# Weight transfers on SyncE's queue, and two streams of preparation for the second MLP

## The chip, the cores and the metric

One core of a Trainium2 chip runs the kernel. The metric is device time in microseconds (us), the median of several executions. The engines: TensorE (PE in the profile; PEld is its weight load), VectorE (DVE), ScalarE (ACT), GpSimd (POOL) and SyncE (SP), which only issues transfers. A small q behind an engine's name (ACTq, SPq) marks its sequencer, which issues DMAs and waits.

## The reference

```python
p_packed = sm_attn(p, k, v)            # 8 batches, 8 heads, 32 packed rows over 576 keys, d = 64
out = sm_attn(q, p_packed, p_packed)   # 576 queries over the 32 packed rows
x = out.transpose(0, 2, 1, 3).reshape(4608, 512)
h = x @ w_in;  g = h * sigmoid(h);            x = g @ w_out        # first MLP, 512 -> 2048 -> 512
h = x @ w_in2; g = h * clip(h + 3, 0, 6) / 6; return g @ w_out2    # second MLP, same sizes
```

All of it is float32. The kernel gets float32 accuracy out of faster matmuls: it splits each operand into a high and a low float32r part and adds three products.

## The kernel before

**Blocks.** The 4608 tokens are nine blocks (j = 0 to 8) of 512. For blocks 1 to 7 the hidden layer of the first MLP is computed from the attention weights and from "fused" weights (packed values times w_in, `fuse_steps`, L607), whose products run beside the blocks before: each step takes one product out of a PSUM bank (L616 to L618), and ScalarE (L622) and VectorE (L623) split it. In each block (`block`, L854) a loop over the 16 columns f of the hidden layer does twelve or six matmuls (L827 to L829), the Silu gate on ScalarE (L835), a split of it by ScalarE (gh, L842) and VectorE (gl, L843), and the projection of the column two before (L850 to L852). Attention steps for later blocks are placed among these by a planner (`Plan`), by costs and due times. A block ends with its sums being copied out of PSUM and stored (x1d, L896).

**Weights.** Block 0 converts the first MLP's weights from raw words (`Feed`: L173, L174 on ScalarE, L179, L180 on VectorE, L185 and a split on GpSimd) and keeps them in DRAM as w1i and w1o. Later blocks load them: wi tiles (`next_in`, L215) with five buffers, wo tiles (`next_out`, L228) with three. ScalarE issues both. The attention's loads (nat, tails of q, k and v, p), x1d and xtd are issued by SyncE.

**Preparation.** `Prep` (L243) makes the second MLP's weights in Strassen-like form: 32 units, each with two loads of raw words (L263), two conversions (L173, L174), bit work on VectorE (L179, L180), an addition on GpSimd (L292), four VectorE sums (L295 to L298), two rounding copies on ScalarE (L300, L301), two subtractions on GpSimd (L303, L304), and three stores to w2 (L308 to L310). ScalarE issues loads and stores. It is a generator: `prep.step()` does the work up to the next `yield`. A unit has nine of them, some with nothing between. `nxt` calls it from block 1 on: twice per column in blocks 1 to 6 (32 steps a block), 46 times in block 7 and 62 times in block 8.

**The second MLP** (`Second`, L918) follows block 8. Its weight loads (ws) and its first x loads (xr) are issued by SyncE; the first of them in block 8.

Every engine works through its own list of instructions in the order of the program, and waits where an operand or a buffer isn't ready. All DMAs take eight landing counters in turn, whichever queue issues them: a DMA waits on its issuing engine until the one eight before it has landed.

Of the kernel before, what the change touches and what calls it, by code (L numbers as in the profile page):

```python
# [1 line left out]

# [6 lines left out]
F32 = mybir.dt.float32  # L9
I32 = mybir.dt.int32  # L10
U32 = mybir.dt.uint32
F32R = mybir.dt.float32r
# [6 lines left out]
def tile_pack_attention_two_mlps(ctx: ExitStack, tc, q, k, v, p, w_in1, w_out1, w_in2, w_out2, out):  # L19
# [8 lines left out]
    nc = tc.nc  # L28
# [141 lines left out]
    def conv_begin(key, room=ring):  # L170
        raw = raws.pop(key).rearrange("p (f t) -> p f t", t=2)
        r, t = room(), room().bitcast(I32)
        nc.scalar.mul(out=r, in_=f32(raw[:, :, 1]), mul=2.0 ** -112)  # L173
        nc.scalar.mul(out=t, in_=raw[:, :, 0].bitcast(U32), mul=2.0 ** -29)  # L174
        raws[key] = raw[:, :, 1], r.bitcast(I32), t
# [32 lines left out]
    def piece_in(f):  # L208
        return w1i[f // GF][:, :, :, f % GF, :].rearrange("c p n f -> p n c f")
# [5 lines left out]
    def next_in():  # L215
        if want_in:
            key = want_in.pop(0)
            t = wts.tile([P, 2, DM], F32R, tag="wi", name="wi", bufs=5)
            if len(key) == 3:
                j, g, c = key  # L220
                nc.scalar.dma_start(out=f32(t).rearrange("p n (i f) -> p n i f", i=GF), in_=w1i[g][c])
            else:
                nc.scalar.dma_start(out=f32(t).rearrange("p n (c f) -> p n c f", c=KC), in_=piece_in(key[1]))
            have_in[key] = t

    projected = [-1, -1]
# [1 line left out]
    def next_out():  # L228

        now, projected[1] = projected[1], -1 if kept else projected[0]  # L230
        while want_out and now >= NF - 2 and (want_out[0][0] * NF + want_out[0][1]) // 2 <= (now + 1) // 2 - 1 + WO:
            j, f = want_out.pop(0)
            t = half_w("out", f)
            nc.scalar.dma_start(out=f32(t), in_=w1o[f].rearrange("n p f -> p n f"))
            have_out[j, f] = t


# [5 lines left out]
    class Prep:  # L243


        def __init__(self, pool, w_in, w_out_):
            self.pool = pool
            self.src = {"in": lambda f: win_src(w_in, f), "out": lambda f: wout_src(w_out_, f)}
            self.units = [(kind, f, h) for kind in ("in", "out") for f in range(HF) for h in range(2)]
            self.steps = self.all()  # L250

        def room(self):
            return self.pool.tile([P, T], F32, tag="pring", name="pr", bufs=4)

        def load(self, u):

            kind, f, h = self.units[u]
            raw = self.pool.tile([P, 2 * T], I32, tag="praw", name="praw", bufs=2)
            for n, to in enumerate(raw.rearrange("p (n r) -> n p r", n=2)):
                src = self.src[kind](f + n * HF)  # L260
                if kind == "out":
                    src = src.rearrange("p a (r f) -> p (a r) f", r=4)
                nc.scalar.dma_start(out=to.rearrange("p (r f) -> p r f", r=2), in_=src[:, h:4:2])  # L263
            raws["p", u] = raw

        def step(self):
            next(self.steps, None)

        def end(self):
            for _ in self.steps:  # L270
                pass

        def all(self):
            self.load(0)
            for _ in range(6):
                yield
            for u, (kind, f, h) in enumerate(self.units):
                key = "p", u
                c = self.pool.tile([P, 8, P], F32, tag="c8", name="c8")
                hi = self.pool.tile([P, S7, P], F32, tag="hi7", name="hi7", bufs=2)  # L280
                conv_begin(key, self.room)
                yield
                yield
                conv_bits(key)
                yield
                if u + 1 < len(self.units):
                    self.load(u + 1)
                yield
                x, r = (t.rearrange("p (n r f) -> p n r f", n=2, r=2) for t in raws.pop(key))
                a = c[:, 0:4].bitcast(I32)  # L290
                a = a.rearrange("p (n r) f -> p n r f", n=2) if kind == "in" else a.rearrange("p (r n) f -> p n r f", n=2)
                nc.gpsimd.tensor_add(out=a, in0=x, in1=r)  # L292
                yield

                nc.vector.tensor_add(out=c[:, 4], in0=c[:, 2], in1=c[:, 3])  # L295
                nc.vector.tensor_sub(out=c[:, 6], in0=c[:, 0], in1=c[:, 2])
                nc.vector.tensor_sub(out=c[:, 5], in0=c[:, 4], in1=c[:, 0])
                nc.vector.tensor_sub(out=c[:, 7], in0=c[:, 1], in1=c[:, 5])  # L298
                yield
                nc.scalar.copy(out=hi[:, 0:2].bitcast(F32R), in_=c[:, 0:2])  # L300
                nc.scalar.copy(out=hi[:, 2:7].bitcast(F32R), in_=c[:, 3:8])  # L301
                yield
                nc.gpsimd.tensor_sub(out=c[:, 0:2].bitcast(F32R), in0=c[:, 0:2], in1=hi[:, 0:2])  # L303
                nc.gpsimd.tensor_sub(out=c[:, 3:8].bitcast(F32R), in0=c[:, 3:8], in1=hi[:, 2:7])  # L304
                yield
                yield
                to = w2[kind][f].rearrange("s p f -> p s f")
                nc.scalar.dma_start(out=to[:, :, h * P:(h + 1) * P], in_=hi)  # L308
                nc.scalar.dma_start(out=to[:, 0:2, (2 + h) * P:(3 + h) * P], in_=c[:, 0:2])
                nc.scalar.dma_start(out=to[:, 2:7, (2 + h) * P:(3 + h) * P], in_=c[:, 3:8])  # L310


    AHEAD = 3
# [3 lines left out]
    def load_tail(n, what):  # L317
        src = {"k": k, "q": q, "v": v}[what]
        b, h0 = n // QPB, (n % QPB) * HQ
        if n == 1 and what != "v":  # L320
            t = half_kb(n, f"{what}t")[0:TAIL, 0:HQ * D].rearrange("p (h d) -> p h d", h=HQ)
        else:
            t = at.tile([TAIL, HQ, D], F32, tag=f"{what}t", name=f"{what}t")
        nc.sync.dma_start(out=t, in_=src[b, h0:h0 + HQ, T:S, :].rearrange("h s d -> s h d"))
        nat[what, n] = t

    def load_nat(n, what, j):
        src = {"k": k, "q": q, "v": v}[what]
        b, h0 = n // QPB, (n % QPB) * HQ + 2 * j
        m = half_kb(n, "nat", 2 * AHEAD, what)  # L330
        rows = src[b, h0:h0 + 2, 0:T, :]
        if what == "v":
            m = m.rearrange("p (h i d) -> p h i d", h=2, i=NI)
            nc.sync.dma_start(out=m.rearrange("p h i d -> p h (i d)"), in_=rows.rearrange("h (p i) d -> p h (i d)", i=NI))
        elif n >= 4:

            g = m.rearrange("p (i b d) -> p i b d", i=NI, b=NI)
            for h in range(2):
                for e in range(2):
                    o = (2 * h + e) * NP  # L340
                    nc.sync.dma_start(out=g[o:o + NP], in_=rows[h].rearrange("(b r i) d -> r i b d", b=NI, i=NI)[:, :, :, e * NP:(e + 1) * NP])
        else:
            m = m.rearrange("p (i h d) -> p i h d", h=2, i=NI)
            for h in range(2):
                nc.sync.dma_start(out=m[:, :, h, :], in_=rows[h].rearrange("(p i) d -> p i d", i=NI))
            m = m.rearrange("p i h d -> p i (h d)")
        nat[what, n, j] = m
# [10 lines left out]
    def spread_p(n):  # L358
        if ("pbd", n) in st:
            return  # L360
        pn = nat.pop(("p", n))
        pbd = at.tile([P, HQ, D], F32, tag="pbd", name="pbd")
        nc.gpsimd.tensor_tensor(out=pbd, in0=pn.to_broadcast([P, HQ, D]), in1=mask.to_broadcast([P, HQ, D]), op=ALU.mult)
        st["pbd", n] = pbd
# [904 lines left out]
    d2s[1] = spare_raw()[:, 0:S]  # L1269
    feed.ahead = RAW - 2  # L1270

    load_nat(0, "k", 0)
    load_tail(0, "q")
    feed.load()
    load_p(0)
    load_tail(0, "k")
    spread_p(0)
    load_nat(0, "k", 1)
    load_tail(1, "q")
    load_tail(1, "k")  # L1280
# [73 lines left out]
    for j in range(NBLK):  # L1354
# [34 lines left out]

        if j == 1:  # L1390
            first_block.close()
            prep = Prep(opened(first_left, "prep"), w_in2, w_out2)
        if j == NBLK - 1:
            first_right.close()
# [4 lines left out]
        def nxt(f, full, j=j):  # L1399
            if j == 0:  # L1400
                if full:
                    feed.advance()
                    calls[0] += 1
                    if 20 <= calls[0] < 25:
                        next_in()
                else:
                    feed.begin()
            else:
                if j >= B - 1 or full:
                    prep.step()  # L1410
                if full and j == B:
                    mlp2.begin_step()
# [52 lines left out]
```

## Time and profile before

| | |
|---|---|
| median of 3 runs | 1669.15 us (1660.82 to 1673.3) |
| profiled execution | 1664.09 us, span 1662.3 us, mean granted clock 0.982 |
| TensorE, VectorE, ScalarE, GpSimd busy | 1559.9, 1047.3, 806.2, 215.1 us |
| transfers by queue | q1 250.68 MB (50.6% of the DMA engines' time), q10 135.81 MB (25.9%) |
| start; block 0 | 0 to 46; to 176.5 us |
| blocks 1 to 8 | to 298, 400.5, 486.5, 589, 695.5, 763.5, 830.5, 924.5 us |
| second MLP | 924.5 to 1662.3 us |

Busy time of an engine is the time in which an instruction of it runs; issuing and waiting don't count. The granted clock is the share of 2.4 GHz that TensorE got. The bounds of the blocks are the ends of the copies of their sums.

### The profile page before, as it was taken

Reading aid. Unit: us, or ns where it says so; the run is one execution under the profiler, and the core shown is the slowest. Engines: PE = TensorE matmul, PEld = TensorE weight load, DVE = VectorE, ACT = ScalarE, POOL = GpSimd, SP = SyncE. Lnnn points to the kernel's source line nnn. Section 1 sums busy time; section 2 is a strip of 40 time slices with the busy share of each in tenths; the row PEclk is TensorE's granted clock in tenths of the full one; section 3 lists DMA queues with packets and bytes.
Section 4 is the critical chain, followed back from the end, with each engine's and each line's share of the span. In section 5 each row is a group of like instructions: output and inputs, shape, how many; then the busy total and the mean of one; then the engine's idle time right before and its main releaser. Section 6 shows DMA issues by size and latency. Waiting matters only on the chain.

```text
span 1662.3 us, 23562 instructions
## 1 busy us (share of the span) xinstructions
PE 1559.9 (94%) x8396; PEld 1339.8 (81%) x8396; DVE 1047.3 (63%) x1750; ACT 806.2 (48%) x1356; POOL 215.1 (13%) x188
## 2 busy tenths in 40 slices
PE   5888899889998999999999999999999999999997
PEld 3566666567676777668878999999999999999997
DVE  5678454655556545664443579579578678687675
ACT  4776444545455444555434345345344444453443
POOL 2455011101111112112223000000000000000000
PEclk9999999999998999999999999999999999999999
DMA  7888695867676764856598687888887888888885
GB/s 195 265 258 276 196 233 151 250 192 212 158 217 188 205 188 116 270 174 210 179 307 264 210 267 252 253 299 253 262 290 252 270 285 253 278 272 253 262 255 166
DMA packets 409750, 388.01 MB, mean 233 GB/s; under 512 B 156193, under 2 KB 282145, under 8 KB 409633
## 3 DMA queue, kind: packets, MB, share of 16 engines
q1 hardware_dynamic: 281200, 250.68, 50.6%
q10 hardware_dynamic: 128432, 135.81, 25.9%
q8 instruction: 68, 1.11, 0.3%
q14 instruction: 50, 0.40, 0.1%
HBM read 324.53 MB, written 61.87 MB: 232 GB/s over the span
## 4 chain that ended last, share of the span: by engine, by line
PE 57%; DVE 17%; ACT 14%; DMA 6%; issue 3%; ACTq 2%; POOL 1%; SPq 0%; DVEq 0%; POOLq 0%
PE b L1169 6%; PE b L1170 6%; PE b L1168 6%; PE acc L850 6%; PE acc L851 5%; PE acc L852 5%; ACT hr L1029 4%; DVE g L1032 4%; PE hps L827 3%; PE hps L829 3%; PE hps L828 3%; PE b L1086 2%; PE b L1084 2%; PE b L1085 2%; DVE fused L623 1%
## 5 line engine op out<-in xcount | busy, mean ns | idle before, releaser
L1169 PE MATMUL b<-ro,ws 128*128 128x384 f32 x672 | 226.5, 337 | 6.2 <-DVE ro L1128 6.2
L1084 PE MATMUL b<-xc,ws 128*128 128x384 f32 x672 | 228.9, 341 | 3.0 <-DVE hv L1048 2.1
L1170 PE MATMUL b<-ro,ws 128*128 128x384 f32 x672 | 225.9, 336 | 0.0
L1168 PE MATMUL b<-ro,ws 128*128 128x384 f32 x672 | 225.8, 336 | 0.0
L1086 PE MATMUL b<-xc,ws 128*128 128x384 f32 x672 | 225.0, 335 | 0.0
L1085 PE MATMUL b<-xc,ws 128*128 128x384 f32 x672 | 224.7, 334 | 0.0
L843 DVE TENSOR_TENSOR gl<-hps,gh 128x512 fp32r<-128x512 f32 x144 | 99.0, 687 | 188.6 <-ACT gh L842 185.5
L1123 ACT CAST ro<-g 128x768 fp32r<-128x768 f32 x168 | 138.3, 835 | 101.9 <-DVE g L1117 36.6
L1128 DVE TENSOR_TENSOR ro<-g,ro 128x768 fp32r<-128x768 f32 x168 | 158.5, 951 | 8.9 <-ACT ro L1123 7.5
L1169 PEld LDWEIGHTS b<-ro,ws 128*128 128x128 f32 x672 | 126.3, 188 | 8.1 <-DVE ro L1128 8.1
L1084 PEld LDWEIGHTS b<-xc,ws 128*128 128x128 f32 x672 | 126.2, 188 | 7.3 <-DVE hv L1048 4.4
L835 ACT ACTIVATE hps<-hps 128x512 f32<-128x512 f32 x144 | 84.0, 583 | 92.6 <-PE hps L829 74.8
L1085 PEld LDWEIGHTS b<-xc,ws 128*128 128x128 f32 x672 | 126.3, 188 | 0.0
L1170 PEld LDWEIGHTS b<-ro,ws 128*128 128x128 f32 x672 | 126.3, 188 | 0.0
L1168 PEld LDWEIGHTS b<-ro,ws 128*128 128x128 f32 x672 | 126.3, 188 | 0.0
L1086 PEld LDWEIGHTS b<-xc,ws 128*128 128x128 f32 x672 | 126.1, 188 | 0.0
L850 PE MATMUL acc<-gh,wr 128*128 128x512 f32 x288 | 119.4, 414 | 1.3 <-ACT gh L842 1.3
L850 PE MATMUL acc<-gh,wo 128*128 128x512 f32 x288 | 117.0, 406 | 2.3 <-ACT gh L842 2.3
L851 PE MATMUL acc<-gl,wr 128*128 128x512 f32 x288 | 114.7, 398 | 0.2 <-DVE gl L843 0.2
L852 PE MATMUL acc<-gh,wr 128*128 128x512 f32 x288 | 114.2, 397 | 0.0
L851 PE MATMUL acc<-gl,wo 128*128 128x512 f32 x288 | 113.4, 394 | 0.2 <-DVE gl L843 0.2
L852 PE MATMUL acc<-gh,wo 128*128 128x512 f32 x288 | 113.3, 393 | 0.0
(262 smaller groups left out, 3048.1 us busy)
## 6 DMA issues: line engine op xcount, KB each, us to landing
ws<-w2in SPq DMA_DIRECT2D x336, 256.0 KB, 4.1
ws<-w2out SPq DMA_DIRECT2D x336, 256.0 KB, 3.4
wi<-w1i ACTq DMA_DIRECT2D x80, 512.0 KB, 4.8
wo<-w1o ACTq DMA_DIRECT2D x64, 512.0 KB, 5.2
x1d<-x SPq DMA_DIRECT2D x18, 512.0 KB, 2.9
w1i<-win SPq DMA_DIRECT2D x16, 512.0 KB, 6.0
praw<-in_moe_w_in_dram ACTq DMA_DIRECT2D x32, 256.0 KB, 5.5
praw<-in_moe_w_out_dram ACTq DMA_DIRECT2D x32, 256.0 KB, 4.8
```

The costliest lines, as they stand in the source:

```text
L843: nc.vector.tensor_sub(out=gl, in0=g, in1=f32(gh))
L850: mm(acc[e], lhsT=w[:, 0, s], rhs=gh, start=first, stop=False)
L851: mm(acc[e], lhsT=w[:, 0, s], rhs=gl, start=False, stop=False)
L852: mm(acc[e], lhsT=w[:, 1, s], rhs=gh, start=False, stop=last)
L1084: mm(ps, lhsT=wh, rhs=xs[k][:, 0, c], start=first, stop=False, skip_group_check=True)
L1085: mm(ps, lhsT=wh, rhs=xs[k][:, 1, c], start=False, stop=False, skip_group_check=True)
L1086: mm(ps, lhsT=wl, rhs=xs[k][:, 0, c], start=False, stop=last, skip_group_check=True)
L1123: nc.scalar.copy(out=t[:, 0], in_=self.operand(s))
L1128: nc.vector.tensor_sub(out=t[:, 1], in0=self.operand(s), in1=f32(t[:, 0]))
L1168: mm(acc[i], lhsT=wh, rhs=ro[:, 0, f], start=first, stop=False, skip_group_check=True)
L1169: mm(acc[i], lhsT=wh, rhs=ro[:, 1, f], start=False, stop=False, skip_group_check=True)
L1170: mm(acc[i], lhsT=wl, rhs=ro[:, 0, f], start=False, stop=last, skip_group_check=True)
```

## The change

All transfers of weights that ScalarE issued after block 0's raw loads (wi, wo, the raw words and the stores of the preparation) are issued by SyncE. wi has four buffers instead of five, and block 0 asks for four tiles early instead of five. The preparation is two generators, one for the even and one for the odd units, with buffers of their own; `step` advances them in turn. A unit still has nine `yield`s, now each with something between them. The preparation begins with block 2 and takes two more steps per column in block 7 (78 in all). The first loads at the start have another order, p first, and the tail of q gets a second buffer.

```diff
 def next_in():
-            t = wts.tile([P, 2, DM], F32R, tag="wi", name="wi", bufs=5)
+            t = wts.tile([P, 2, DM], F32R, tag="wi", name="wi", bufs=4)
-                nc.scalar.dma_start(out=f32(t).rearrange("p n (i f) -> p n i f", i=GF), in_=w1i[g][c])
+                nc.sync.dma_start(out=f32(t).rearrange("p n (i f) -> p n i f", i=GF), in_=w1i[g][c])
...
 def next_out():
-            nc.scalar.dma_start(out=f32(t), in_=w1o[f].rearrange("n p f -> p n f"))
+            nc.sync.dma_start(out=f32(t), in_=w1o[f].rearrange("n p f -> p n f"))
...
 class Prep:
-            self.steps = self.all()
-
-        def room(self):
-            return self.pool.tile([P, T], F32, tag="pring", name="pr", bufs=4)
+            self.steps = [self.all(first) for first in range(2)]
+            self.turn = 1
...
-            raw = self.pool.tile([P, 2 * T], I32, tag="praw", name="praw", bufs=2)
+            raw = self.pool.tile([P, 2 * T], I32, tag=f"praw{u % 2}", name="praw")
...
-                nc.scalar.dma_start(out=to.rearrange("p (r f) -> p r f", r=2), in_=src[:, h:4:2])
+                nc.sync.dma_start(out=to.rearrange("p (r f) -> p r f", r=2), in_=src[:, h:4:2])
...
         def step(self):
-            next(self.steps, None)
+
+            self.turn = 1 - self.turn
+            next(self.steps[self.turn], None)
...
-        def all(self):
-            self.load(0)
-            for _ in range(6):
+        def all(self, first):
+            room = lambda: self.pool.tile([P, T], F32, tag=f"pring{first}", name="pr", bufs=2)
+            mine = range(first, len(self.units), 2)
+            self.load(first)
+            for _ in range(4):
                 yield
...
-                conv_begin(key, self.room)
-                yield
+                conv_begin(key, room)
                 yield
                 conv_bits(key)
                 yield
-                if u + 1 < len(self.units):
-                    self.load(u + 1)
-                yield
+                if u + 2 < len(self.units):
+                    self.load(u + 2)
...
                 nc.vector.tensor_sub(out=c[:, 6], in0=c[:, 0], in1=c[:, 2])
+                yield
                 nc.vector.tensor_sub(out=c[:, 5], in0=c[:, 4], in1=c[:, 0])
...
                 nc.gpsimd.tensor_sub(out=c[:, 0:2].bitcast(F32R), in0=c[:, 0:2], in1=hi[:, 0:2])
+                yield
                 nc.gpsimd.tensor_sub(out=c[:, 3:8].bitcast(F32R), in0=c[:, 3:8], in1=hi[:, 2:7])
                 yield
+                to = w2[kind][f].rearrange("s p f -> p s f")
+                nc.sync.dma_start(out=to[:, :, h * P:(h + 1) * P], in_=hi)
+                nc.sync.dma_start(out=to[:, 0:2, (2 + h) * P:(3 + h) * P], in_=c[:, 0:2])
+                nc.sync.dma_start(out=to[:, 2:7, (2 + h) * P:(3 + h) * P], in_=c[:, 3:8])
                 yield
-                yield
-                to = w2[kind][f].rearrange("s p f -> p s f")
-                nc.scalar.dma_start(out=to[:, :, h * P:(h + 1) * P], in_=hi)
-                nc.scalar.dma_start(out=to[:, 0:2, (2 + h) * P:(3 + h) * P], in_=c[:, 0:2])
-                nc.scalar.dma_start(out=to[:, 2:7, (2 + h) * P:(3 + h) * P], in_=c[:, 3:8])
...
-    load_nat(0, "k", 0)
-    load_tail(0, "q")
-    feed.load()
     load_p(0)
     load_tail(0, "k")
+    load_tail(0, "q")
+    load_nat(0, "k", 0)
     spread_p(0)
+    feed.load()
...
         if j == 1:
             first_block.close()
+        if j == 2:
             prep = Prep(opened(first_left, "prep"), w_in2, w_out2)
...
-                    if 20 <= calls[0] < 25:
+                    if 20 <= calls[0] < 24:
                         next_in()
...
-                if j >= B - 1 or full:
+                if j > 1 and (j >= B - 1 or full):
+                    prep.step()
+                if j == B - 1 and full:
                     prep.step()
```

## Rows read from the trace of the kernel before

**Rows 1.** Busy time by stretch: bounds, length, engines (instructions), clock, DMA share, GB/s.
```profile
176.50:298.00 121.50, 107.94 (x609) 74.91 (x608) 58.92 (x124) 57.24 (x98) 14.90 (x17) 0.97 0.77 206
298.00:400.50 102.50, 91.04 (x465) 67.18 (x464) 57.69 (x114) 52.85 (x91) 13.60 (x12) 0.95 0.75 211
400.50:486.50 86.00, 84.75 (x461) 63.75 (x460) 47.89 (x101) 44.98 (x79) 16.56 (x17) 1.00 0.66 178
486.50:589.00 102.50, 91.92 (x460) 67.22 (x459) 57.30 (x114) 51.84 (x89) 13.08 (x12) 0.93 0.76 209
...
695.50:763.50 68.00, 65.11 (x278) 49.86 (x278) 40.49 (x74) 36.07 (x58) 8.38 (x7) 0.97 0.63 201
763.50:830.50 67.00, 67.00 (x295) 54.83 (x294) 25.70 (x53) 33.65 (x60) 20.07 (x17) 1.00 0.63 201
830.50:924.50 94.00, 89.91 (x386) 72.81 (x385) 35.76 (x65) 38.48 (x65) 23.05 (x18) 0.98 0.85 261
924.50:1662.30 737.80, 719.92 (x4172) 712.56 (x4170) 539.98 (x799) 324.30 (x515) 14.18 (x6) 1.00 0.81 260
```

**Rows 2.** TensorE's waits, blocks 1 to 8: releaser, us in total, times, longest.
```profile
PE hps L827 <- DVE gl L843: 9.3, 4, 4.6
PE abank L616 <- issue: 9.3, 6, 2.9
PE acc L850 <- ACT gh L842: 3.6, 2, 2.3
PE abank L406 <- ACT gh L842: 3.5, 1, 3.5
...
PE abank L478 <- DVE ppf L465: 2.7, 2, 1.9
PE abank L616 <- DVE gl L843: 2.6, 1, 2.6
...
PE abank L461 <- DVE a1Tt L104: 1.6, 1, 1.6
PE hps L827 <- DVE xh L623: 1.5, 1, 1.5
```

**Rows 3.** ScalarE's timeline early in block 2: start, length, idle time before.
```profile
298.99 0.38 ACTq L308 DMA_DIRECT2D w2in<-hi  x1
299.46 1.36 ACTq L309 DMA_DIRECT2D w2in<-c  x1
300.91 1.24 ACTq L310 DMA_DIRECT2D w2in<-c  x1
302.19 0.66 ACT L173 ACTIVATE pr<-praw 128x512 f32<-128x512 f32 x1 [2.63 <-issue]
...
303.30 0.56 ACT L622 CAST fused<-abank 64x512 fp32r<-64x512 f32 x1
```

**Rows 4.** ScalarE's waits, blocks 1 to 8.
```profile
ACT pr L173 <- issue: 37.3, 17, 4.9
...
ACT hi L301 <- DVE c L298: 20.3, 18, 1.4
...
ACT gh L842 <- DMA w2out<-c: 3.6, 1, 3.6
```

**Rows 5.** GpSimd's instructions of the preparation, by tile: ns shortest/median/longest.
```profile
L292 POOL TENSOR_TENSOR c<-pr x32: 1263/1288/1782, 206.6 to 907.6; 128x512 int32<-128x512 int32 x32
...
L304 POOL TENSOR_TENSOR c<-c,hi x32: 1548/1569/2092, 222.6 to 910.8; 128x640 fp32r<-128x640 f32 x32
```

**Rows 6.** SyncE's own waits, whole span.
```profile
SPq L324 <- PE abank L461: 94.6, 10, 17.8
```

**Rows 7.** DMA issues of the page: count, KB each, median us to landing.
```profile
wi<-w1i ACTq DMA_DIRECT2D x80, 512.0 KB, 4.8
wo<-w1o ACTq DMA_DIRECT2D x64, 512.0 KB, 5.2
```

**Rows 8.** TensorE's waits in the start, 0 to 46 us.
```profile
PE abank L372 <- POOL pbd L363: 9.1, 1, 9.1
```

More of the change, by code (lines that the diff above doesn't have):

```diff
@@ L1 @@
 from contextlib import ExitStack
+from itertools import zip_longest
 import concourse.bass as bass
@@ L217, in next_in @@
             key = want_in.pop(0)
-            t = wts.tile([P, 2, DM], F32R, tag="wi", name="wi", bufs=5)
+            t = wts.tile([P, 2, DM], F32R, tag="wi", name="wi", bufs=4)
             if len(key) == 3:
                 j, g, c = key
-                nc.scalar.dma_start(out=f32(t).rearrange("p n (i f) -> p n i f", i=GF), in_=w1i[g][c])
+                nc.sync.dma_start(out=f32(t).rearrange("p n (i f) -> p n i f", i=GF), in_=w1i[g][c])
             else:
-                nc.scalar.dma_start(out=f32(t).rearrange("p n (c f) -> p n c f", c=KC), in_=piece_in(key[1]))
+                nc.sync.dma_start(out=f32(t).rearrange("p n (c f) -> p n c f", c=KC), in_=piece_in(key[1]))
             have_in[key] = t
@@ L262, in load @@
                     src = src.rearrange("p a (r f) -> p (a r) f", r=4)
-                nc.scalar.dma_start(out=to.rearrange("p (r f) -> p r f", r=2), in_=src[:, h:4:2])
+                nc.sync.dma_start(out=to.rearrange("p (r f) -> p r f", r=2), in_=src[:, h:4:2])
             raws["p", u] = raw
         def step(self):
-            next(self.steps, None)
+            self.turn = 1 - self.turn
+            next(self.steps[self.turn], None)
         def end(self):
-            for _ in self.steps:
+            for both in zip_longest(*self.steps):
                 pass
-        def all(self):
-            self.load(0)
-            for _ in range(6):
+        def all(self, first):
[3 more added lines that the diff above has]
+            for _ in range(4):
                 yield
-            for u, (kind, f, h) in enumerate(self.units):
+            for u in mine:
+                kind, f, h = self.units[u]
                 key = "p", u
-                c = self.pool.tile([P, 8, P], F32, tag="c8", name="c8")
-                hi = self.pool.tile([P, S7, P], F32, tag="hi7", name="hi7", bufs=2)
-                conv_begin(key, self.room)
-                yield
+                c = self.pool.tile([P, 8, P], F32, tag=f"c8{first}", name="c8")
+                hi = self.pool.tile([P, S7, P], F32, tag=f"hi7{first}", name="hi7")
+                conv_begin(key, room)
                 yield
@@ L285, in all @@
                 yield
-                if u + 1 < len(self.units):
-                    self.load(u + 1)
-                yield
-                x, r = (t.rearrange("p (n r f) -> p n r f", n=2, r=2) for t in raws.pop(key))
+                if u + 2 < len(self.units):
+                    self.load(u + 2)
+                r, t = (v.rearrange("p (n r f) -> p n r f", n=2, r=2) for v in raws.pop(key))
                 a = c[:, 0:4].bitcast(I32)
                 a = a.rearrange("p (n r) f -> p n r f", n=2) if kind == "in" else a.rearrange("p (r n) f -> p n r f", n=2)
-                nc.gpsimd.tensor_add(out=a, in0=x, in1=r)
+                nc.gpsimd.tensor_add(out=a, in0=r, in1=t)
                 yield
@@ L322, in load_tail @@
         else:
-            t = at.tile([TAIL, HQ, D], F32, tag=f"{what}t", name=f"{what}t")
+            t = at.tile([TAIL, HQ, D], F32, tag=f"{what}t", name=f"{what}t", bufs=2 if what == "q" else 1)
         nc.sync.dma_start(out=t, in_=src[b, h0:h0 + HQ, T:S, :].rearrange("h s d -> s h d"))
```

## The prediction

> **What bounds the kernel now.** I first read the stretches block by block [rows 1]. The second MLP (924.5 to 1662.3 us) keeps TensorE at full clock and 98% busy, and the change touches nothing that it issues; I leave it at 738 us. Block 0 and the start change in details only. So the question is the 748 us of blocks 1 to 8. There the reader is to see two kinds of blocks. Blocks 3 and 7 are full: 84.75 us busy of 86, 67.00 of 67. Blocks 1, 2, 4, 6 and 8 are not: TensorE is busy 107.94 of 121.5, 91.04 of 102.5, 91.92 of 102.5, 65.11 of 68 and 89.91 of 94, and the granted clock there is 0.97, 0.95, 0.93, 0.97 and 0.98, a mixture of the two levels of 1.2 and 2.4 GHz. Idle time is 13.6 + 11.5 + 10.6 + 2.9 + 4.1 = 42.7 us in these five, and the clock loses (1 - c) times the stretch, 3.6 + 5.1 + 7.2 + 2.0 + 1.9 = 19.8 us. This is the whole pot: some 62 us.
>
> Next the waits of TensorE in these blocks [rows 2]: none is for a transfer. It waits for ScalarE and VectorE: to have a PSUM bank emptied, or an operand split. The group of 9.3 us at L616 with the releaser "issue" names nobody, so I went to the times of its six cases and read ScalarE's timeline before each. The largest one stands for the pattern [rows 3]: from 298.99 ScalarE issues the three stores of a preparation unit, 0.38, 1.36 and 1.24 us, converts the next raw tile, and only then, at 303.30, evicts the bank that the next product of the fused weights needs; TensorE had nothing to do for 2.9 us, the longest case of that group. Then ScalarE's own waits [rows 4]: it stood 37.3 us before L173, the first instruction behind those stores, because of its own issuing, and 20.3 us before L301 for a VectorE instruction that the preparation had issued one step earlier. Both queues share eight landing counters, each of which must be down before it is used again, so ScalarE also stood for transfers of others: 3.6 us before a Silu's split for the landing of a store.
>
> **The change part by part.** (1) *Issuing leaves ScalarE.* In blocks 1 to 8 ScalarE issues wi, wo, the raw tiles and the stores; an issue costs it 0.38 to 1.36 us in [rows 3]. I price it by TensorE's idle time behind it, group by group [rows 2]: L616 behind issuing 9.3; L616 behind gl 2.6 (gl behind a Silu's split that stood for the landing of xtd); L850 behind gh 3.6 (the split that stood for a store, in block 8 [rows 4]); L406 behind gh 3.5 (in block 1, behind three wo issues in a row); L827 behind xh 1.5. Sum 20.5 us. Of the 9.3 us at L827 behind gl, the two long cases, up to 4.6, come out of a VectorE chain that starts behind such a ScalarE stall; I take a third, 3 us.
>
> (2) *Preparation leaves block 1.* A unit took nine steps, now it takes nine of its stream's, and the streams alternate; block 1 had 32 steps, so some 3.5 units of 32 go elsewhere. Their conversions stood directly ahead of L461 behind a1Tt (1.6) and of the 1.9 of the 2.7 us behind ppf [rows 2]: 3.5 us, nothing takes their place.
>
> (3) *The clock.* The low stretches in blocks 1, 2, 4, 6 and 8 follow idle times of 2.3 to 4.6 us. I take half of the 19.8 us, 9.9, since about half of the long idle times are among those of (1).
>
> (4) *What is late next.* With ScalarE on time, the bank still waits for VectorE's half of the split, and VectorE is already second in the list of waits. In the pattern of [rows 3] the eviction could have begun 2.5 us sooner and the gap was 2.93, so a sixth remains there; where chains are longer more does. I give back a third of (1) and (3), (20.5 + 3 + 9.9) / 3 = 11.1 us.
>
> (5) *Denser preparation in block 7.* Steps there go from 46 to 78: about 3.6 units more. A unit's two long GpSimd instructions take 1.29 and 1.57 us [rows 5], with the short one some 3.6 in all; ScalarE spends on a unit four conversions like the 0.66 us of L173 [rows 3], some 2.5, and VectorE about as much. Block 7 has 20.07 us of GpSimd, 33.65 of ScalarE and 25.70 of VectorE in 67 [rows 1], so 13, 9 and 9 us more fit beside TensorE. A step now comes every 67 / 78 = 0.86 us and one of the same stream every 1.7 us, about as long as the longest GpSimd instruction, so an in-order VectorE may stand for it; Silu's split runs two columns of work ahead and covers that. Bounds: 0, and 13 us if TensorE paid for all of GpSimd; I take 1. Counted out, the two streams need 2 x (4 + 16 x 9) = 296 steps and there are 5 x 32 + 78 + 62 = 300, so nothing is left over at the end of block 8.
>
> (6) *SyncE takes the transfers.* It must keep its order, and it does stand still, up to 17.8 us for one load of a tail [rows 6]. What counts is whether it comes to a weight transfer later than ScalarE did. The eight landing counters are taken in turn in program order, which gives the order of both queues' transfers; laid out so, SyncE had passed the transfer ahead of a wi load too late in 7 of 80 cases [rows 7], by at most an estimated 2.1 us. These waits are for things at the same place of the program, and ScalarE comes there last. The second buffer for q's tail removes one more such wait. Cost 0. (7) *wi with four buffers instead of five, four early loads instead of five:* a load lands in 4.8 us [rows 7] and is asked for four fused products ahead, which stand some 6 us apart in block 2 and 5.9 us in block 8; 0, and if that cover went, one landing for each of the two places where g turns. (8) *The start:* TensorE's first instruction waits 9.1 us for the block-diagonal p [rows 8], whose load now is issued first instead of fifth. But the next transposes need k's second half, which keeps its place in the queue, and ScalarE converts a raw tile whose load now comes later. Bounds: 0 and 5; I take a gain of 1.
>
> Sum: 20.5 + 3 + 3.5 + 9.9 - 11.1 - 1 + 1 = 25.8 us. The profiled execution took 1664.1 us (span 1662.3), so 1638.3. The median of the runs stands 5.1 us above it; on that scale the forecast is 1669.15 - 25.8 = **1643**. Its own range: with nothing given back 1632, with two thirds given back 1655.
>
> The Trainium skill, page "DMA: Bandwidth & Descriptors", section "Issuing engines are not separate DMA queues", says that issuing from several engines only saves sequencer time, usually small against the transfer. The trace agrees on the size (0.38 to 1.36 us against a landing of 4.8), yet shows that time ahead of evictions; by the rule read alone the change would be worth almost nothing.
>
> **The rivals.** *VectorE takes over* (18%): ScalarE gets its time back, but the same evictions now wait for gl and the fused split. For it: VectorE releases L827 for 9.3 us, and blocks 1, 2 and 4 have 57 to 59 us of its work [rows 1]. Then two thirds of (1) and nearly all of (3) stay: 3.5 + 23.5 / 3 = 11, or 1658. *The whole pot* (15%): idle times go together, and the clock with them; two thirds of 62 us plus what blocks 0 and 5 give, 45 us: 1624. For it: block 3 has the same attention load per window and runs 100% full. Against it: blocks 2 and 4 alone have twelve fused products each to split.
>
> *SyncE is late* (7%), the case on the other side: weights of the next block stand behind x1d's stores, which go out only when the last copy of a block is made. If wo or wi then came a landing late at each of eight turns of blocks, TensorE would lose 8 x 5.2 [rows 7] = 42 us, against 26 gained: 16 slower, 1669 + 16 = 1685. It decides from the point where SyncE comes to a load later than its buffers reach ahead, about 15 us for wo's three; the 2.1 us of (6) speak against it. The Trainium skill, same page, section "Queues, rings and completion order", has each transfer engine take turns between queues by packet; by that rule small loads lose their own turn beside 512 KB weights and land later. No run here shows it yet; it would make the late case likelier, and I count it there. That the change does not do what it says has none either: the issuing engine is written out in each line.
>
> **How the numbers follow.** Forecast 60%, whole pot 15%, VectorE 18%, late SyncE 7%. About 1% is what a measurement of this kernel can tell from no change, that is below 1652.5 or above 1685.8 us. Faster: the forecast but for its upper edge (56%) and the whole pot, 71%; same: that edge, VectorE and half of the late case, 25%; slower 4%. The range, 1618 to 1661, takes in the forecast with its bounds, most of the whole pot and VectorE's case, and leaves out the late one.
>
> **What would show it.** ScalarE's waits at L173 for issuing and at L301 for L298 are gone, and TensorE's at L616 with them; the span's clock rises from 0.982 to about 0.99. Blocks shorten by some 7 (1), 6.5 (2), 6 (4), 2.5 (6) and 3.5 (8) us; 3 and the second MLP stay within 1; block 7 grows by at most 2. I am wrong if TensorE's waits name a DMA or SyncE's order in blocks 1 to 8, if blocks 2 and 4 keep their length though ScalarE's stalls are gone, or if block 7 grows by several us.

## The result, and the profile after

The changed kernel takes 1642.17 us, the median of four runs (1641.17 to 1646.81), the kernel before 1668.71: 26.5 us less by the medians. The ratio on record, estimated over the runs and not from the two medians, is 0.9857 with a 95% interval of 0.9818 to 0.9896, so 17 to 30 us less. The forecast was 1643. The experiments show that this sum hides errors of opposite sign.

The execution that was profiled is the longest of the four, 1646.81 us, and has the lowest mean clock; the others had spans of 1639.4 to 1640.6 us at 0.983 to 0.986. Its span is only 17.3 us shorter than that of the profile before, so its blocks add up to less than the 26.5 us. From the changed kernel's page: span, the two queues (packets, MB, share of the DMA engines), and the chain that ended last; then that chain's line of before.

```profile
span 1645.0 us, 23735 instructions
q1 hardware_dynamic: 400752, 372.34, 74.4%
q10 hardware_dynamic: 8880, 14.16, 2.6%
PE 63%; DVE 16%; ACT 12%; issue 4%; DMA 3%; POOL 1%; SPq 1%; ACTq 0%; DVEq 0%; POOLq 0%
```
```profile
PE 57%; DVE 17%; ACT 14%; DMA 6%; issue 3%; ACTq 2%; POOL 1%; SPq 0%; DVEq 0%; POOLq 0%
```

ScalarE's queue (q10) is down to block 0's raw loads, and its sequencer is gone from the chain, where it had 2%. Block 0 to the second MLP in the changed kernel, by stretch (columns as in [rows 1]):

```profile
46.00:180.10 134.10, 118.53 (x572) 88.01 (x572) 96.13 (x127) 90.59 (x163) 64.14 (x49) 0.92 0.83 252
180.10:299.90 119.80, 110.17 (x609) 77.72 (x608) 52.22 (x106) 51.62 (x86) 4.56 (x8) 0.94 0.66 179
299.90:398.70 98.80, 91.18 (x465) 68.37 (x464) 58.05 (x110) 51.82 (x89) 10.83 (x10) 0.93 0.72 208
398.70:487.70 89.00, 85.42 (x462) 63.77 (x461) 47.04 (x99) 45.69 (x82) 14.70 (x16) 1.00 0.64 176
487.70:580.20 92.50, 86.58 (x458) 63.60 (x457) 60.92 (x119) 50.23 (x87) 15.98 (x14) 1.00 0.76 210
580.20:667.00 86.80, 85.56 (x460) 63.92 (x459) 49.25 (x103) 45.66 (x82) 17.84 (x17) 1.00 0.69 186
667.00:751.00 84.00, 79.54 (x342) 61.14 (x341) 52.66 (x93) 46.44 (x77) 9.67 (x8) 0.98 0.66 210
751.00:819.20 68.20, 68.20 (x301) 55.85 (x300) 37.23 (x75) 40.61 (x74) 33.54 (x28) 1.00 0.85 261
819.20:906.10 86.90, 85.77 (x380) 70.85 (x379) 40.00 (x66) 37.34 (x65) 22.63 (x18) 1.00 0.96 292
906.10:1645.00 738.90, 720.17 (x4173) 712.75 (x4171) 540.12 (x799) 324.33 (x516) 14.18 (x6) 1.00 0.80 260
```

Three more rows of before by the same view: block 0, and blocks 5 and 6. The bound of these two stands at 695.5 us in the table above, which is when SyncE got to store the sums; they had been copied by 678.2, so [rows 1] has too short a block 6. To the tenth the copies of the other blocks end at 486.2 (3), 588.8 (4), 763.4 (6), 830.1 (7) and 924.3 us (8); the gains below go by these.

```profile
46.00:176.50 130.50, 113.10 (x568) 84.27 (x567) 96.36 (x125) 89.59 (x161) 63.81 (x49) 0.96 0.86 263
588.80:678.20 89.40, 86.41 (x460) 63.84 (x459) 47.95 (x101) 45.78 (x81) 15.19 (x16) 1.00 0.60 168
678.20:763.40 85.20, 80.23 (x342) 60.74 (x341) 52.33 (x96) 46.70 (x77) 11.93 (x10) 0.98 0.66 204
```

Block by block the gain is 1.7 (1), 3.7 (2), -3.3 (3), 10.1 (4), 2.6 (5), 1.2 (6), -1.5 (7) and 7.3 us (8). The forecast had 7, 6.5, within 1, 6, none named, 2.5, at worst -2, and 3.5. Block 0 is 3.6 us longer though TensorE idles less in it (15.6 against 17.4 us): its clock was 0.92 instead of 0.96. Waits of TensorE, blocks 1 to 8 of the changed kernel, as in [rows 2]; its line numbers are four higher.

```profile
PE hps L831 <- DVE gl L847: 7.8, 2, 4.6
PE abank L482 <- DVE ppf L469: 4.4, 3, 3.0
PE abank L620 <- issue: 4.2, 2, 3.6
PE abank L560 <- DVE a2t L538: 3.8, 2, 2.6
PE abank L376 <- POOL pbd L367: 3.2, 1, 3.2
PE acc L854 <- DMA wo<-w1o: 3.1, 1, 3.1
```

The waits behind ScalarE's held splits are gone (L850 and L406 behind gh, L616 behind gl), and the product's wait at L616, now L620, is down from 9.3 to 4.2 us. Two are new, the last two: the block-diagonal p and wo's landing, both in block 1. Of ScalarE's waits in the changed kernel, the line that answers to L301 of [rows 4]:

```profile
ACT hi L304 <- DVE c L301: 13.9, 8, 4.9
```

The line for L173 behind issuing (37.3 us) has no successor. The wait at L304 was foretold to go; it is down from 20.3 us only to 13.9.

### The profile page after: what moved, and what is told of

It reads as the page before. It is cut to its first block, busy times and chain, and to the rows that moved or that the text cites. A ratio compares the mean times of both kernels' runs of the same rounds, so it can differ in the third digit from the quotient of the medians.

```text
span 1645.0 us, 23735 instructions
## 1 busy us (share of the span) xinstructions
PE 1559.4 (95%) x8396; PEld 1343.5 (82%) x8396; DVE 1059.6 (64%) x1750; ACT 804.1 (49%) x1356; POOL 216.5 (13%) x188
## 4 chain that ended last, share of the span: by engine, by line
PE 63%; DVE 16%; ACT 12%; issue 4%; DMA 3%; POOL 1%; SPq 1%; ACTq 0%; DVEq 0%; POOLq 0%
PE acc L854 7%; PE b L1173 6%; PE b L1174 6%; PE b L1172 6%; PE acc L855 6%; PE acc L856 6%; ACT hr L1033 4%; PE hps L831 4%; DVE g L1036 4%; PE hps L833 4%; PE hps L832 3%; PE b L1090 2%; PE b L1088 2%; PE b L1089 2%; DVE ro L1132 1%
## 5 line engine op out<-in xcount | busy, mean ns | idle before, releaser
L854 PE MATMUL acc<-gh,wr 128*128 128x512 f32 x288 | 119.8, 416 | 0.0
```

The costliest lines, as they stand in the source:

```text
L854: mm(acc[e], lhsT=w[:, 0, s], rhs=gh, start=first, stop=False)
```

## The experiments

All medians stand beside runs of the kernel before on the same chip, whose own median lay between 1667.8 and 1669.6 us; each ratio is to these.

**The queue alone, and everything but the queue.** The first is the kernel before with this edit on every weight transfer, and with the second buffer for q's tail; the second is the changed kernel with the edit turned back.

```diff
-                nc.scalar.dma_start(...)   # wi, wo, praw, w2 stores
+                nc.sync.dma_start(...)
```

> The kernel before with the queue part alone: wi, wo, the raw words and the stores of the preparation are issued by SyncE, and q's tail has its second buffer (with one, SyncE would wait for itself). One stream, old timetable, five wi buffers, old start. Theory A, issuing was what held ScalarE and through it TensorE: most of the gain is here, 14 to 20 us below the kernel before, the product's wait at L616 for issuing under 3 us. Theory B, the gain is the spacing and the timetable of the preparation: within 5 us of the kernel before, and ScalarE's wait at L301 still some 20 us.

> The changed kernel with the queue part undone: ScalarE issues wi, wo, the raw words and the stores again; two streams, new timetable, new start and four wi buffers stay. Theory A: only the 3.5 us of block 1 and the start are left, 3 to 8 us below the kernel before, and TensorE still waits some 8 us or more at the fused product for issuing. Theory B: 18 us or more below the kernel before.

Measured: the queue alone 1633.75 us (1631.99 to 1635.27), ratio 0.9791 (0.9774 to 0.9808), 35.5 us less than before and better than the whole change. Streams, timetable and start on ScalarE's queue: 1688.64 us, ratio 1.0118 (1.0100 to 1.0136), 19 us *slower* than before. Theory A has the direction and theory B falls, but both runs lie outside what A gave: the queue gave twice as much, and the rest by itself costs where A had a small gain (TensorE's wait at the product for issuing is 6.1 us there, not 8 or more). Blocks 2, 4 and 8 with the queue alone:

```profile
299.20:391.10 91.90, 87.97 (x465) 65.67 (x464) 57.45 (x114) 52.77 (x91) 13.13 (x12) 0.98 0.86 246
475.70:568.60 92.90, 87.81 (x460) 65.27 (x459) 57.62 (x114) 51.77 (x89) 13.12 (x12) 0.98 0.83 229
804.10:891.40 87.30, 87.29 (x387) 72.06 (x386) 37.06 (x66) 37.67 (x65) 23.04 (x18) 1.00 0.92 281
```

They lose 10.6, 9.7 and 6.9 us against before, and the clock is back at 0.98 to 1.00. Waits in its blocks 1 to 8, three of TensorE and one of ScalarE:

```profile
PE hps L827 <- DVE gl L843: 7.0, 3, 3.7
PE abank L372 <- POOL pbd L363: 3.7, 1, 3.7
...
PE abank L616 <- issue: 1.8, 2, 1.2
```
```profile
ACT hi L301 <- DVE c L298: 22.5, 20, 1.9
```

ScalarE's wait at L301 is as long as before (20.3), and the gain is there all the same: it was no part of the price.

Without the queue, what the denser preparation does to ScalarE is seen in its waits (kernel without the queue part, blocks 1 to 8), and in the lengths of blocks 1 and 7:

```profile
ACT hps L839 <- DMA w2out<-c: 22.9, 3, 11.7
ACT hps L839 <- DMA w2in<-c: 21.5, 4, 6.2
```
```profile
176.70:288.60 111.90, 106.20 (x609) 74.62 (x608) 52.12 (x106) 51.08 (x86) 4.20 (x8) 0.99 0.70 186
...
770.30:853.00 82.70, 75.16 (x304) 58.23 (x303) 40.14 (x75) 40.62 (x75) 33.50 (x28) 0.96 0.70 215
```

Block 1, where no preparation runs now, is 9.6 us shorter than before, with the weights still issued by ScalarE. Every later block but 4 is longer than before. The longest wait, 11.7 us, is put down to the landing of a store. ScalarE's timeline shows what fills it: five of the six stores of two units and a load of wi, issued one behind the other, which alone takes 10.7 us. Two of these stores, and the Silu behind them all:

```profile
858.42 3.12 ACTq L311 DMA_DIRECT2D w2out<-hi  x1
861.59 3.09 ACTq L312 DMA_DIRECT2D w2out<-c  x1
...
866.42 0.58 ACT L839 ACTIVATE hps<-hps 128x512 f32<-128x512 f32 x1 [11.75 <-DMA w2out<-c]
```

**Parts of the queue.** The kernel before with only the preparation's transfers, or only wi and wo, on SyncE: the same edit on those lines alone (q's tail in two buffers).

> The kernel before, and of its transfers the raw words and the stores of the preparation alone go to SyncE (q's tail in two buffers); wi and wo stay with ScalarE. The whole queue part gave 35 us. If the three stores ahead of a conversion are what held ScalarE, as the prediction read the largest waits: 20 us or more of the 35 are here, and ScalarE's wait at L173 for issuing is under 10 us. If the gain is spread over all of ScalarE's transfers: 15 to 20 us.

> The kernel before, and of its transfers wi and wo alone go to SyncE (q's tail in two buffers); the raw words and the stores of the preparation stay with ScalarE. If the stores are the larger part: 10 us or less below the kernel before, with the wait at L173 still at some 35 us. If every issue counts by its length, wi and wo are 144 of 304 transfers in blocks 1 to 8 and carry nearly half: 15 us or more. If the two parts don't add to 35, ScalarE waits for landing counters of the transfers that it keeps.

Measured: the preparation's alone 1650.78 us, ratio 0.9904 (0.9889 to 0.9918), 17 us, as with a gain spread over all transfers, and ScalarE's wait at L173 for issuing is gone; wi and wo alone 1666.83 us, ratio 0.9991 (0.9976 to 1.0006), nothing, with that wait at 28.9 us. Together they gave 35: the parts don't add. With wi and wo alone on SyncE, TensorE waits for them (that kernel, blocks 1 to 8), and block 1 is 10.7 us longer than before, which eats up the 9.3 us that blocks 4, 5, 6 and 8 gain. Of SyncE's own waits in these blocks, the last line is one at the issue of wo:

```profile
PE abank L616 <- DMA wi<-w1i: 7.3, 1, 7.3
PE acc L850 <- DMA wo<-w1o: 6.8, 2, 3.8
```
```profile
177.40:309.60 132.20, 114.97 (x610) 80.33 (x609) 58.46 (x124) 57.41 (x97) 14.96 (x17) 0.91 0.65 172
```
```profile
SPq L234 <- DMA w2in<-hi: 13.2, 2, 7.6
```

Neither wait of TensorE is in the list of before. The wait of SyncE is for the landing of a store that ScalarE issued and that a load of wo doesn't need: there the landing counters, which both queues share, tie one queue to the other. In the queue alone no issue of wo waits more than 0.6 us for a landing. How much of the missing 18 us the counters make is not shown, since no run took them apart.

**The start, and the buffers of wi.** The changed kernel with the old order of the first loads; the queue alone with four wi buffers and four early loads.

```diff
-    load_p(0)
-    load_tail(0, "k")
-    load_tail(0, "q")
     load_nat(0, "k", 0)
-    spread_p(0)
+    load_tail(0, "q")
     feed.load()
+    load_p(0)
+    load_tail(0, "k")
+    spread_p(0)
...
-            t = wts.tile([P, 2, DM], F32R, tag="wi", name="wi", bufs=5)
+            t = wts.tile([P, 2, DM], F32R, tag="wi", name="wi", bufs=4)
-                    if 20 <= calls[0] < 25:
+                    if 20 <= calls[0] < 24:
```

> The changed kernel with the old order of the first loads (q's tail keeps its second buffer). If the start's order is worth what the prediction says: 1 us above the changed kernel, at most 5; first TensorE instruction at about 9 us instead of 3.3. If the first instruction sets the end of the start: 5 us above. If the order harms, since TensorE's early instructions fall apart into more idle times and the clock stays low longer: some 3 us below the changed kernel.

> The queue part alone, with four wi buffers instead of five and four early loads. The prediction has it at nothing: within 2 us of the run of the queue part alone (1634). If the streams' loss of 8 to 19 us is that of the buffer: 1642 or more, with TensorE waiting for wi's landing at the fused product.

Measured: 1641.55 us (ratio 0.9840, 0.9821 to 0.9859) and 1635.5 us (0.9798, 0.9785 to 0.9812). Neither differs from its partner. The queue alone and the changed kernel with the old start ran side by side on one chip, and their runs don't overlap (1631.99 to 1635.27 against 1640.37 to 1645.79): streams, timetable and four buffers together cost 8 us. Their profiles show where. Block 1 is shorter, 113.7 against 122.2 us; blocks 2 and 3 of the changed kernel with the old start are longer (91.9 and 84.6 us in the queue alone):

```profile
292.10:390.20 98.10, 90.45 (x465) 67.66 (x464) 57.83 (x111) 51.85 (x89) 10.81 (x10) 0.95 0.74 210
390.20:480.30 90.10, 86.73 (x462) 64.64 (x461) 47.20 (x99) 45.69 (x81) 14.69 (x16) 0.98 0.63 174
```

**Streams and timetable.** The changed kernel with the old timetable, and the queue alone with the new one:

```diff
-                if j >= B - 1 or full:
+                if j > 1 and (j >= B - 1 or full):
+                    prep.step()
+                if j == B - 1 and full:
                     prep.step()
```

> The changed kernel with the old timetable of the preparation: it begins with block 1 and takes one step less per column in block 7; both streams and SyncE's queue stay. The prediction's price of the timetable: 2.5 us above the changed kernel (3.5 back in block 1, 1 saved in block 7). Theory B, the timetable carries much of the gain: 8 us or more above. If SyncE's queue is what makes block 1 slow, block 1 gets longer by more, since the preparation's transfers then stand ahead of p and wo there.

> The queue part alone, as before, plus the new timetable of the preparation (from block 2 on, one more step per column in block 7), with one stream, five wi buffers, old start. If the two streams as such are what costs, the timetable's 10 us come on top of the queue part's: about 1623 us, blocks 1 to 8 shorter mainly in block 1. If the gain of the timetable exists only with two streams: 1630 to 1636. If one stream cannot bear 78 steps in block 7, that block grows from 67 to over 72 us.

Measured, all on SyncE's queue:

| | old timetable | new timetable |
|---|---|---|
| one stream | 1633.75 | 1647.07 (ratio 0.9864, 0.9849 to 0.9879) |
| two streams | 1652.62 (0.9901, 0.9885 to 0.9916) | 1641.55 (old start), 1642.17 |

The kernels with one stream have five wi buffers and the old start, the one with two streams and the old timetable has four and the new start; neither of these made a difference above. The timetable is worth 10 us with two streams and costs 13 with one. One stream can't bear 78 steps in block 7; this is that block with one stream and the new timetable:

```profile
741.60:821.80 80.20, 73.32 (x299) 56.98 (x298) 33.71 (x77) 39.83 (x72) 31.93 (x27) 0.97 0.77 228
```

It was 66.7 us with 46 steps, and is 68.2 with two streams. Two streams cost elsewhere. Blocks 2, 4, 5 and 6 with two streams and the old timetable:

```profile
302.40:401.40 99.00, 90.29 (x465) 68.11 (x466) 56.39 (x114) 53.80 (x93) 12.75 (x12) 0.92 0.80 232
...
485.90:582.60 96.70, 88.98 (x460) 65.66 (x459) 61.35 (x119) 52.68 (x91) 15.32 (x14) 0.96 0.78 220
582.60:673.10 90.50, 86.86 (x460) 64.76 (x459) 49.45 (x99) 43.98 (x78) 12.35 (x13) 0.98 0.65 178
673.10:760.40 87.30, 81.61 (x348) 61.98 (x347) 51.20 (x93) 48.48 (x82) 14.34 (x12) 0.98 0.60 189
```

Against the queue alone, with five wi buffers (91.9, 92.9, 85.9 and 82.9 us) or four (94.6, 93.7, 85.9 and 82.9), each is 3 to 7 us longer, and none has the higher clock.

**Is it bursts?** Both streams pass through the same stage in adjacent steps. Here the second is four steps behind.

```diff
-            for _ in range(4):
+            for _ in range(1 + 4 * first):
```

> The changed kernel with the second stream four of its nine steps behind the first, so that the same stage of two units no longer comes in adjacent steps. If the cost of the streams is bursts (two pairs of conversions on ScalarE, two bit steps on VectorE in a row): 4 us or more below the changed kernel (1642). If the cost is the spread of the steps or the buffers: within 3 us of it.

Measured: 1642.98 us, ratio 0.9849 (0.9835 to 0.9862): no difference. It is not the bursts. Up to block 2, where the preparation begins, this kernel is the changed kernel instruction for instruction; its block 1 is not as long for all that (119.8 us at a clock of 0.94 in the profile above):

```profile
177.50:290.70 113.20, 105.76 (x610) 74.34 (x609) 52.21 (x106) 51.45 (x85) 4.20 (x8) 0.99 0.69 188
```

So the length of a single block in a single profile can be off by 6.6 us without any change to the program. Its blocks 2 and 3, with 96.6 and 89.2 us, are near those of the changed kernel.

**Is it the second stream, or the new place of the steps?** The steps of the changed kernel, one stream for 18 units, then two.

```diff
+    SOLO = 18
...
-            self.steps = [self.all(first) for first in range(2)]
+            self.solo = self.all(range(SOLO))
...
+                self.steps = [self.all(range(first, len(self.units), 2)) for first in (SOLO, SOLO + 1)]
```

> The changed kernel with one stream up to the 18th unit (blocks 2 to 6) and two streams for the other 14 (blocks 7 and 8); the steps are those of the changed kernel, all else is its own. If a second stream costs in blocks 2 to 6 and pays in the dense block 7: blocks 2 to 6 as with one stream (92, 85, 93, 86, 83 to 88 us), block 7 at 68 as in the changed kernel, in all some 1630 us. If it is the new place of the yields that costs, not the second stream: blocks 2 and 3 at 98 and 89 us as in the changed kernel, and 1640 us or more.

Measured: 1630.36 us (1627.45 to 1633.81), ratio 0.9772 (0.9757 to 0.9786), 12 us below the changed kernel. Blocks 1, 2, 3 and 7 of this mixed kernel:

```profile
180.10:297.80 117.70, 108.79 (x610) 76.59 (x609) 52.19 (x106) 51.39 (x85) 4.20 (x8) 0.96 0.67 182
297.80:390.00 92.20, 88.54 (x464) 66.10 (x463) 57.28 (x113) 51.86 (x89) 12.50 (x11) 0.97 0.75 211
390.00:475.90 85.90, 85.14 (x461) 63.79 (x460) 49.90 (x101) 44.56 (x79) 15.06 (x16) 1.00 0.73 195
...
736.30:807.50 71.20, 69.38 (x304) 56.22 (x303) 36.93 (x74) 37.67 (x70) 27.87 (x23) 1.00 0.80 252
```

Blocks 2 and 3 are back from 98.8 and 89.0 to 92.2 and 85.9 with the very same steps, and block 7 keeps most of its gain (71.2 us, where 68 were expected). It holds across profiles: with the new timetable and all on SyncE, blocks 2 and 3 take 96.6 to 98.8 and 89.0 to 90.1 us with two streams (three profiles), 92.2 to 93.6 and 85.9 to 86.1 with one (three). So it is the second stream that costs in blocks 2 and 3, and pays where the preparation is dense. By what the second stream costs there (its units are not more, and the busy times of VectorE, ScalarE and GpSimd are the same within 4 us a block) stays open.

**One queue in block 1.** The first try loads p and k's tail a window earlier (one stream, new timetable, four wi buffers); the second takes the mixed kernel and lets ScalarE issue wi and wo in block 1, where no preparation runs.

```diff
-                i = cs.index(c) + 1
+                i = cs.index(c) + 2     # pn, kt: two buffers each
...
+        queue[0] = nc.scalar if j == 1 else nc.sync     # next_in, next_out: queue[0].dma_start
```

> The queue part with the new timetable and one stream, four wi buffers, and p and the tail of k in two buffers each, loaded one window earlier. If small loads behind 512 KB weights in SyncE's one queue hold TensorE early in block 1 (3.2 to 3.7 us idle there, and the clock behind it): that wait is gone and block 1 is 3 to 7 us shorter than with one stream and the old place of these loads. If p would come anyway too late through GpSimd: no difference beyond 2 us.

> The mixed kernel (one stream in blocks 2 to 6, two in 7 and 8), with wi and wo issued by ScalarE in block 1 alone, where no preparation runs. If in block 1 one queue is the harm (p and k's tail land behind five weight tiles, wo comes late): p lands in some 5 us after its issue instead of 8 to 9, TensorE's waits for pbd and for wo's landing are gone there, block 1 takes 112 to 114 us instead of 118, and the whole 1624 to 1627 us. If ScalarE's stalls cost there as much as the order of one queue: within 2 us of the mixed kernel's 1630.

Measured: p early 1644.53 us (ratio 0.9851, 0.9836 to 0.9866), against 1647.07 without it (and with five wi buffers); the intervals overlap. The wait for pbd is gone from block 1, which is 2.9 us shorter (114.6 against 117.5), while a wait of 2.7 us for wo stays. ScalarE in block 1: 1627.89 us (ratio 0.9750, 0.9732 to 0.9768), against 0.9772 of the mixed kernel; again the intervals overlap, and the two profiled spans differ by 1.2 us. Block 1 of it:

```profile
179.80:291.70 111.90, 106.14 (x609) 74.65 (x608) 52.10 (x106) 51.44 (x85) 4.21 (x8) 0.98 0.70 187
```

It is 5.8 us shorter than the mixed kernel's, less than the 6.6 us by which this block varies by itself; blocks 2, 7 and 8 lose 4.4 us again. The waits say more: with wi and wo on ScalarE's queue and no preparation in block 1, those for pbd and wo are gone, here and in the kernel without the queue part, and block 1 takes 111.9 us both times. With all on SyncE and no preparation there, TensorE stands 4.0 to 6.3 us for the two in each of five profiles, and block 1 takes 113.2 to 119.8 us. The same 32 KB load of p early in block 1, from its issue to its landing (shortest/median/longest of one transfer): first in the changed kernel, then with wi and wo on ScalarE's queue in that block.

```profile
DMA to landing us min/median/max: 9.4/9.4/9.4
```
```profile
DMA to landing us min/median/max: 5.2/5.2/5.2
```

In the other kernels with all on SyncE it lands in 7.7 to 10.6 us, in the kernel without the queue part in 5.1, and in the kernel before it took 3.5 us. This last kernel, 41.7 us below the kernel before and 14 below the changed one, has the lowest median of the study, though not clear of the mixed kernel's.

## Why the prediction was right, point by point

**(1), (3), (4): the queue was worth more.** The three together were 20.5 + 3 + 9.9 - 11.1 = 22.3 us; the queue alone gave 35.5, with four wi buffers 33.9. In the profile of the queue alone TensorE's idle time in blocks 1 to 8 (length less busy time) goes from 48.9 to 28.0 us, and the clock's loss from 19.5 to 7.4; with four buffers to 29.5 and 12.5. The groups were the right ones: of the 23.5 us listed, L616 behind issuing lost 7.5, the four smaller groups all of their 11.2, and L827 behind gl 2.3, together 21.0. The term that was mis-sized is (4), giving back a third, 11.1 us, to VectorE: by the medians nothing was given back. VectorE did not take over; its rival case asked for two thirds. In the whole change much of the clock's gain is lost again: 15.8 us of the 19.5 are still there in its profile, 12.5 and 12.4 in those of the variants with the old start and with the offset. The mean clock of its runs was 0.980 to 0.986 where about 0.99 was foretold.

**(2), (5): a term that was missing.** The forecast had a gain of 3.5 for block 1 and a cost of 1 for block 7. Block 7 was right (1.5). (2) was mis-sized, too: with ScalarE still issuing, block 1 without the preparation is 9.6 us shorter, and with all on SyncE 2.4 to 9.0 shorter than in the queue alone. Against it stands the second stream, which got no price at all in blocks 2 to 6. It costs 17 us at the old timetable (1652.62 against 1635.5 with the same four buffers, by the ratios as well), and at the new one 3.0 to 6.6 in block 2 and 2.9 to 4.2 in block 3, by the profiles of both kinds above. Streams, timetable and start together cost some 8 us where a gain of 3.5 stood. The error of 13 us on the queue and that of 12 on the rest cancel. That the sum came out right is luck; that the gain is the queue's, through ScalarE's issuing, is not.

**(6): SyncE's cost was not nothing.** Its order does hold for the most part: where all transfers go by SyncE, TensorE's waits name a DMA a few times at most. But the prediction called itself wrong if they named one in blocks 1 to 8, and wo's 3.1 us in block 1 do. Together with the 3.2 us behind p they are the late-SyncE rival, in one block of eight; of the block's length this is 1.3 to 7.9 us, by profiles that vary by as much. The estimate looked at when SyncE issues a load, not at what lies ahead of it in the queue. P's load is issued behind two wi and three wo tiles of 512 KB and lands 9.4 us later; with the tiles on the other queue the same load lands in 5.2 us. The Trainium skill, page "DMA: Bandwidth & Descriptors", section "Queues, rings and completion order", has the transfer engines take turns between queues, a rule that the prediction gave no chance of its own. The trace agrees with it as far as these landings go.

**(7), (8): right as far as can be measured.** Four buffers and the new start change nothing that can be told from the spread. TensorE's first instruction comes at 3.3 us instead of 9.1, and then waits for k.

**A reading that was wrong.** That blocks 2 and 4 alone have twelve fused products each to split, an argument against the rival of the whole pot, is not so: block 6 has as many, which its bound in [rows 1] hid. Blocks 7 and 8 have none; the 5.9 us of (7) in block 8 are its columns.

## What to carry to other kernels

An engine that computes should not issue many transfers in the midst of its work: what counts is who stands behind it while it issues and waits, and here TensorE's idle time went down together with the time lost to the low clock. Try such a group as a whole before its parts: here the parts gave 17 us and nothing, the whole 35. Then look for small urgent loads behind big ones in the one queue that is left; two queues there took TensorE's waits away, though the gain on the whole was too small to be sure of. Don't read a single block of a single profile as a cost. And test the parts of a change each by itself, also when the sum comes out as foretold.

## What the runs showed that was not expected

- The same instructions up to block 2 ran in two profiles, of the changed kernel and of the one with the offset, at clocks of 0.92 and 0.95 in block 0 (134.1 and 131.5 us) and of 0.94 and 0.99 in block 1 (119.8 and 113.2 us). Over whole executions the time goes with the clock, too: of the twelve of the kernel with wi and wo alone on SyncE, the shortest took 1656.65 us at 0.985, the longest 1672.15 at 0.975.
- Denser preparation is a matter of who issues it: with the same 78 steps block 7 takes 82.7 us when ScalarE issues and 68.2 when SyncE does; with 46 steps it took 66.7 either way.
